# Attention with 120- and 96-row key tiles, and products over all 128 partitions, ahead of two MoE layers

## Chip, core and metric

One NeuronCore of a Trainium2 chip runs the whole kernel in one launch. The metric is the device time of the launch in microseconds; the times below are the median of three runs and their spread. The engines are named as in the profile: PE is TensorE (matmuls), PEld its weight loads, DVE VectorE, ACT ScalarE, POOL GpSimd, SP SyncE, which issues most DMAs.

## What is computed

The input has 4 batches x 8 heads x 576 tokens x 64 dimensions of q, k and v, and one score `s` per head and token. Only the first third of the reference matters here, the attention:

```python
scores = scale * np.matmul(q, k.transpose(0, 1, 3, 2))
cum = np.cumsum(np.maximum(s, 0.0), axis=-1)
bias = -(cum[:, :, :, None] - cum[:, :, None, :])
scores = np.where(causal, -1000000000.0, scores + np.minimum(bias, 0.0))
scores = scores - np.max(scores, axis=-1, keepdims=True)
attn = np.exp(scores)
attn = attn / (np.sum(attn, axis=-1, keepdims=True) + 1e-09)
return np.matmul(attn, v)
```

Its output goes through an FFN (512 to 2048 to 512), and that through eight experts with a routing of 288 tokens each. Both come after attention and are not touched.

## The kernel before

**Heads and pairs.** `Attention.run` (L383) goes over 33 steps `n`, one per head and one more; two heads are a pair `p`. Step `n` computes the scores and row maxima of head `n`, the values of head `n-1`, and then the exponentials of head `n`. Odd steps are odd heads. The order of the work on every engine is written out by hand: each engine runs its instructions in the order of the code, waiting where an operand is not there yet.

**Operands.** Products are exact to more than one fp32r pass: q is split into a high and a low part, X = (high, low), Z holds the high part and rows for the bias and the maxima, Y and W hold the same of k. `prep_hi` (L191) brings a pair's q or k, both heads side by side, from rows to columns with five transposes on TensorE into the PSUM tile `pt`: one of 64 rows (keys 512 to 575), four of 128 (keys `4a + r` of partition `a`). ScalarE copies the high parts out (L219, L221, L207), VectorE makes the low ones (L230, L233, `prep_lo`). For k a DMA on the GpSimd queue copies the high part to the other half of Y (L211). k of the next pair is prepared in even steps after the fourth score tile, q at the end of even steps.

**Scores and maxima.** `rows_max` (L236) computes six score tiles of up to 448 columns: a product over 128 rows (L249) and one over 96 (L250) each. VectorE takes row maxima (L252, L256) into `m`, one column per tile of queries; the first tile has 64 queries, so rows 64 to 127 of its column keep the zeros of the set-up. `nm` is made of them in two steps (L258, L259). `rows_put` (L262, "the put") turns the maxima into rows with five products against the identity (L271), one per tile of queries, the first over 64 rows, and ScalarE copies them into Z (L272). The PSUM tiles of scores, exponentials and put share four buffers in turn (tag `s`).

**Exponentials and values.** `exps` (L275) recomputes the scores by key tiles, with masks as products (`mu`), and ScalarE writes exp of them to E (L305). `values` (L313) multiplies E with V and a block of ones, key tile by key tile, in fp32, which gives two products per call (L333). The last key tile has 64 keys; its rows of E and V are cut to 64. The order in a step is: score tiles 1 to 4, then (odd steps) the first two value blocks, score tiles 5 and 6, more values, the put, the values of key tiles 3 and 4, then the exponentials.

**Loads.** `load` (L166) fetches q, k and v of four heads at a time on the SP queue, some 5 heads ahead, spread over steps: for q and k four DMAs of 512 rows (128 partitions x 4 rows) and one of 64 rows of all four heads.

**Beside it.** The FFN's weights come as 64-bit numbers. `Ffn.side` (L526) converts one block per step: two steps on DVE (L494, L495), one on ACT (L498), two on DVE (L500, L502), one on ACT (L504), a multiply on POOL (L505), a DMA to DRAM (L523). These stand in the same queues as attention's work.

**Set-up.** `setup` (L58) fills constants, among them the ones in V on GpSimd (L119), ahead of GpSimd's first copy into Z (L149).

Of the kernel before, what the change touches and what calls it, by code (L numbers as in the profile page):

```python
# [33 lines left out]
class Attention:  # L34
# [23 lines left out]
    def setup(self, identf):  # L58
        nc, c = self.nc, self.c
        S = self.S  # L60
        self.identf = identf
        st = self.w.tile([32, S], F32, name="s_in", tag="El")
        nc.scalar.dma_start(st, self.s.rearrange("b h s -> (b h) s"))
        self.load_first(0)
        zero = c.tile([128, 128], F32, name="zero")
        one = c.tile([128, 1], F32, name="one")
        nc.vector.memset(zero, 0.0)
        nc.vector.memset(one, 1.0)
        self.identb = c.tile([128, 128], BF16, name="identb")
        nc.vector.tensor_copy(self.identb, identf)  # L70

        self.ml = c.tile([128, 576], BF16, name="ml")
        self.mu = c.tile([128, 128], BF16, name="mu")
        nc.gpsimd.memset(self.ml[:, :448], 0.0)
        nc.gpsimd.affine_select(self.ml[:, 448:], zero, pattern=[[-1, 128]], compare_op=OP.is_ge, fill=-1e30,
                                base=0, channel_multiplier=1)
        nc.gpsimd.affine_select(self.mu, zero, pattern=[[1, 128]], compare_op=OP.is_ge, fill=-1e30,
                                base=0, channel_multiplier=-1)
        self.stacks, self.vbuf, self.mcol = [], [], []
        for i in range(2):  # L80
            X = c.tile([128, 2, S], F32R, name=f"X{i}")
            Y = c.tile([128, 2, 640], F32R, name=f"Y{i}")
            Z = c.tile([128, 2, S], F32R, name=f"Z{i}")
            W = c.tile([128, 2, 640], F32R, name=f"W{i}")
            V = c.tile([128, 5, 2, 3, 64], F32, name=f"V{i}")
            m = c.tile([128, 6], F32, name=f"m{i}")
            self.stacks.append((X, Y, Z, W))
            self.vbuf.append(V)
            self.mcol.append(m)
            nc.vector.memset(m, 0.0)  # L90

        zb, ob = zero[:, 0:1], one
        dve = lambda o, x: nc.vector.tensor_copy(o, x)
        gps = lambda o, x: nc.gpsimd.memset(f(o), 0.0 if x is zb else 1.0)

        def fill(o, x, cp):
            if cp is not gps:
                r = o.shape
                x = x[o.start_partition():o.start_partition() + r[0]]
                x = (x[:, :, None] if len(r) == 3 else x).to_broadcast(list(r))  # L100
            cp(o, x)

        act = lambda o, x: nc.scalar.activation(o, x, AF.Copy)

        def fill_w(i):
            X, Y, Z, W = self.stacks[i]
            for o, x, cp in ((W[64:128], zb, act), (W[96:98, :, :S], ob, act), (Y[:, :, S:], zb, dve),
                             (W[0:64, :, S:], zb, dve)):
                fill(o, x, cp)

        def fill_z(i, cp):
            Z = self.stacks[i][2]
            for o, x in ((Z[64:128], zb), (Z[64:66], ob)):
                fill(o, x, cp)

        fill_w(0)
        fill_z(0, gps)
        for V in self.vbuf:
            nc.gpsimd.memset(V[:, :, :, 1], 1.0)  # L119
        self.prep_hi(0, 1)  # L120
        self.prep_hi(0, 0)
        cum = self.w.tile([32, S], F32, name="cum", tag="El")
        nc.vector.tensor_scalar(st, st, 0.0, None, op0=OP.max)
        nc.vector.tensor_tensor_scan(cum, st, st, 0.0, op0=OP.add, op1=OP.bypass)
        ck = self.w.tile([32, 2, S], F32R, name="ck", tag="Eh")
        nc.vector.tensor_copy(ck[:, 0], cum)
        nc.vector.tensor_tensor(ck[:, 1], cum, f(ck)[:, 0], op=OP.subtract)
        X, Y, Z, W = self.stacks[0]
        for h in range(2):
            nc.sync.dma_start(f(W)[64:66, h, :S], f(ck)[h:h + 1])  # L130
        self.ckd = self.dr.tile([32, 2, S], F32, name="ckd")
        nc.sync.dma_start(self.ckd, f(ck))
        self.load_first(1)
        self.first_pair(0)
        fill_z(1, gps)
        fill_w(1)
        self.identr = c.tile([128, 128], F32R, name="identr")
        nc.vector.tensor_copy(self.identr, identf)
        for j in range(10, 15):
            self.load(0, j)  # L140

        self.rd = self.dr.tile([self.B * self.H, S], F32, name="rd")
# [11 lines left out]
    def load_first(self, p):  # L154

        for name in "kq":
            if p == 0:
                t = self.ld.tile([128, 5, 4, 64], F32, name="n" + name)
                self.nat[name, 0] = t[:, :, 0:2]
                self.nat[name, 1] = t[:, :, 2:4]  # L160
            t, s = self.nat[name, p], getattr(self, "qs" if name == "q" else name)[0, 2 * p:2 * p + 2]
            for h in range(2):
                self.nc.sync.dma_start(t[:, 0:4, h], s[h, 0:512].rearrange("(p r) d -> p r d", r=4))
            self.nc.sync.dma_start(t[:64, 4], s[:, 512:576].rearrange("h p d -> p h d"))

    def load(self, g, j):  # L166

        nc = self.nc
        if 2 * g >= self.NP:
            return  # L170
        name, r = "kqv"[j // 5], j % 5
        b, h0 = divmod(4 * g, self.H)
        s = getattr(self, "qs" if name == "q" else name)[b, h0:h0 + 4]
        if name == "v":
            rows = s[:, r * 128:min(r * 128 + 128, self.S)]
            t = self.vbuf[g % 2][:rows.shape[1], r]
            for i in range(2):
                nc.sync.dma_start(t[:, i, 0::2], rows[2 * i:2 * i + 2].rearrange("h p d -> p h d"))
            return
        if r == 0:  # L180
            t = self.ld.tile([128, 5, 4, 64], F32, name="n" + name)
            self.nat[name, 2 * g] = t[:, :, 0:2]
            self.nat[name, 2 * g + 1] = t[:, :, 2:4]
            self.nt = t
        t = self.nt
        if r == 4:
            nc.sync.dma_start(t[:64, 4], s[:, 512:576].rearrange("h p d -> p h d"))
        else:
            nc.sync.dma_start(t[:, 0:4, r], s[r, 0:512].rearrange("(p r) d -> p r d", r=4))

    def prep_hi(self, p, which):  # L191

        nc, S = self.nc, self.S
        x = self.nat["qk"[which], p]
        pt = self.pt[which] = self.ps.tile([128, 1024], F32, name="pt", tag="t" if p or which else "o")
        nc.tensor.transpose(pt[:, 512:576], x[:64, 4].rearrange("p h d -> p (h d)"),
                            self.identf[:64, :64])
        for r in range(4):
            nc.tensor.transpose(pt[:, 0:512].rearrange("p (a r) -> p r a", r=4)[:, r, :],  # L199
                                x[:, r].rearrange("p h d -> p (h d)"), self.identf)  # L200
        if p == 0:
            return
        X, Y, Z, W = self.stacks[p % 2]
        self.copy_hi(p, which, (0, 1))
        if which == 0:
            for h in range(2):
                nc.scalar.activation(Z[0:64, h], self.pt[0][64 * h:64 * h + 64, :S], AF.Copy,  # L207
                                     scale=1.0 / math.sqrt(self.D))
        else:
            nc.gpsimd.dma_start(f(W)[64:66, :, :S], self.ckd[2 * p:2 * p + 2].rearrange("h r s -> r h s"))  # L210
            nc.gpsimd.dma_start(f(Y)[64:128, :, :S], f(Y)[0:64, :, :S])  # L211

    def copy_hi(self, p, which, heads):
        nc, S = self.nc, self.S
        X, Y, Z, W = self.stacks[p % 2]
        for h in heads:
            src = self.pt[which][64 * h:64 * h + 64, :S]
            if which == 0:
                nc.scalar.activation(X[0:64, h], src, AF.Copy, scale=1.0 / math.sqrt(self.D))  # L219
            else:  # L220
# [2 lines left out]
    def prep_lo(self, p, which, heads=(0, 1)):  # L223
# [1 line left out]
        nc, S = self.nc, self.S  # L225
        X, Y, Z, W = self.stacks[p % 2]
        for h in heads:
            src = self.pt[which][64 * h:64 * h + 64, :S]
            if which == 0:
                nc.vector.scalar_tensor_tensor(X[64:128, h], src, 1.0 / math.sqrt(self.D), f(X)[0:64, h],  # L230
                                               op0=OP.mult, op1=OP.subtract)
# [30 lines left out]
    def rows_put(self, n, nm):  # L262
# [3 lines left out]
        for q0, tiles in ((0, self.QT[:4]), (448, self.QT[4:])):  # L266
            t = self.ps.tile([128, 512], F32, name="pr", tag="s", bufs=4)
            for a, b in tiles:
                i = self.QT.index((a, b))
                m = b - a  # L270
                nc.tensor.matmul(t[:2, a - q0:b - q0], nm[:m, i, :], self.identr[:m, :m], start=True, stop=True)  # L271
            nc.scalar.activation(Z[96:98, n % 2, q0:b], t[:2, :b - q0], AF.Copy)  # L272


# [38 lines left out]
    def values(self, n, mid=None):  # L313
# [6 lines left out]
        for (g0, g1), order in zip(((0, 256), (256, 576)), self.VALUES):  # L320
# [3 lines left out]
            for i, w in enumerate(order):  # L324
                if w == "|":
                    if mid:
# [3 lines left out]
                a, b = self.KT[kb]  # L330
                c0 = max(a, g0)
                e0 = self.ECOL[kb] + c0 - a
                nc.tensor.matmul(t[:, 256 + c0:256 + g1], V[:b - a, kb, 64 * h:64 * h + 128],  # L333
                                 E[:b - a, e0:e0 + g1 - c0], start=i == 0, stop=i == len(order) - 1)
        self.evac = lambda: self.out(n, t)
        if n < 2 * self.NP - 1:
            self.evac()
# [1315 lines left out]
```

## Time and profile before

| | |
|---|---|
| median of 3 runs | 1049.25 us (1046.25 to 1054.68) |
| the profiled execution | 1042.44 us |
| its span, first to last instruction | 1040.7 us |
| mean granted clock of TensorE | 0.98 of full speed |
| TensorE busy (matmuls) | 968.7 us, 93% |
| VectorE busy | 790.0 us, 76% |
| ScalarE, GpSimd busy | 489.3 us (47%), 455.1 us (44%) |

All durations come from the one profiled execution. "Busy" is the time in which an engine has an instruction under way; matmuls overlap each other, and their ends are modelled, so the distance from start to start says more than a duration. A weight load can run while the matmul ahead of it streams. A row of the time order has the start, the duration, the engine, the line, output and inputs, and in brackets the idle time ahead and what ended it; x2 is two instructions that follow each other. Attention is the first 289 us of the span.

### The profile page before, as it was taken

The page shows a single profiled execution, that of the slowest core. Times are in us where ns is not written, and L with a number is a line of the kernel's source. Part 1 is how long each engine was busy: PE and PEld are TensorE (multiplying, and loading weights), DVE is VectorE, ACT ScalarE, POOL GpSimd, SP SyncE. Part 2 cuts the span into 40 slices and gives each one's busy share as a digit, 9 for nine tenths or more (in the row PEclk, how much of TensorE's full clock was granted, in tenths as well). Part 3 has the DMA queues.
Part 4 walks back from the last instruction along what each step waited for, and adds up shares of the span by engine and source line. Part 5 has one row for each costly group of instructions (what it writes and reads, how often), then busy time and mean ns, then how long its engine had stood idle before and what let it go on. Part 6 is the DMA issues. An engine that isn't in the chain of part 4 may idle for free.

```text
span 1040.7 us, 18588 instructions
## 1 busy us (share of the span) xinstructions
PE 968.7 (93%) x6479; PEld 856.2 (82%) x6479; DVE 790.0 (76%) x2029; ACT 489.3 (47%) x961; POOL 455.1 (44%) x471
## 2 busy tenths in 40 slices
PE   6899999999989999999899899999899979989996
PEld 5777777777768899888798798889788878879996
DVE  6688888988857667999999999885576687766510
ACT  5677777777745532322322322430245435536531
POOL 3245454445423233424424333330668868973211
PEclk9999999999999999999899899999899989999999
DMA  5767777878566040020020110101645455557400
GB/s 129 166 163 200 184 205 188 218 189 214 165 212 232 2 172 1 1 91 1 6 87 1 53 39 0 62 1 42 198 136 164 132 169 166 167 147 236 127 24 24
DMA packets 123067, 122.66 MB, mean 118 GB/s; under 512 B 73922, under 2 KB 90562, under 8 KB 122844
## 3 DMA queue, kind: packets, MB, share of 16 engines
q1 hardware_dynamic: 104604, 89.79, 30.8%
q0 software_dynamic: 17312, 30.55, 10.1%
q10 hardware_dynamic: 1056, 1.12, 0.4%
q8 instruction: 51, 0.84, 0.3%
q14 instruction: 44, 0.36, 0.1%
HBM read 89.36 MB, written 27.50 MB: 112 GB/s over the span
## 4 chain that ended last, share of the span: by engine, by line
PE 66%; DVE 22%; issue 5%; DMA 3%; ACT 2%; POOL 2%; SPq 0%; another core or an unknown queue 0%; POOLq 0%; DVEq 0%; ACTq 0%
PE ph L619 11%; PE py L1486 8%; PE ph L1434 8%; DVE junk L677 7%; PE po L333 6%; PE pst L301 6%; PE px L656 4%; PE px L658 4%; PE px L657 4%; PE ps L249 2%; DVE cmp L1212 2%; PE ps L250 2%; PE rp L1121 2%; PE pt L199 2%; DVE nm L259 2%
## 5 line engine op out<-in xcount | busy, mean ns | idle before, releaser
L641 POOL TENSOR_TENSOR gl<-u,gh 128x384 fp32r<-128x384 f32 x80 | 98.4, 1230 | 237.1 <-ACT gh L640 152.6
L1212 POOL TENSOR_TENSOR wl<-raw,wh 128x512 fp32r<-128x512 f32 x98 | 129.4, 1346 | 59.6 <-DMA raw<-in_moe_w_dram 33.8
L628 ACT ACTIVATE u<-u,half 128x384 f32<-128x384 f32 x96 | 59.2, 617 | 183.4 <-DVE u L627 180.9
L619 PE MATMUL ph<-xh,ih 128*128 128x384 f32 x384 | 132.2, 344 | 7.4 <-ACT xh L605 4.2
L619 PE MATMUL ph<-xl,ih 128*128 128x384 f32 x384 | 132.4, 345 | 4.1 <-DVE xl L606 4.1
L619 PE MATMUL ph<-xh,il 128*128 128x384 f32 x384 | 132.3, 345 | 3.0 <-DVE il L591 2.9
L677 DVE SCALAR_TENSOR_TENSOR junk<-wt,gb 128x512 f32<-128x512 f32 x128 | 116.7, 947 | 0.0
L333 PE MATMUL po<-E,V 128*128 128x320 f32 (+4 forms) x448 | 112.6, 379 | 0.4 <-ACT E L305 0.4
L677 DVE SCALAR_TENSOR_TENSOR junk<-x,gb 128x512 f32<-128x512 f32 x120 | 103.0, 888 | 4.5 <-ACT x L665 4.5
L656 PE MATMUL px<-oh,gh 128*128 128x512 f32 x240 | 96.0, 400 | 1.7 <-ACT x L665 1.7
L658 PE MATMUL px<-oh,gl 128*128 128x512 f32 x240 | 96.6, 402 | 0.7 <-POOL gl L641 0.7
L657 PE MATMUL px<-ol,gh 128*128 128x512 f32 x240 | 95.4, 398 | 0.0
L333 PEld LDWEIGHTS po<-E,V 128*128 128x128 f32 (+1 forms) x448 | 74.9, 191 | 20.1 <-issue 7.4
L619 PEld LDWEIGHTS ph<-xh,ih 128*128 128x128 f32 x384 | 73.5, 192 | 13.8 <-ACT xh L605 5.9
L1486 PE MATMUL py<-hh,wh 128*128 128x288 f32 x256 | 81.1, 317 | 0.0
L619 PEld LDWEIGHTS ph<-xl,ih 128*128 128x128 f32 x384 | 73.7, 192 | 8.7 <-DVE xl L606 5.2
L1212 ACT ACTIVATE wh<-raw 128x512 fp32r<-128x512 f32 x128 | 76.0, 623 | 9.2 <-DMA raw<-in_moe_w_dram 8.3
L1434 PE MATMUL ph<-xh,wh 128*128 128x288 f32 x256 | 79.1, 309 | 0.2 <-ACT xh L1212 0.2
L1434 PE MATMUL ph<-xl,wh 128*128 128x288 f32 x256 | 78.5, 307 | 0.5 <-DVE xl L1212 0.4
L1434 PE MATMUL ph<-xh,wl 128*128 128x288 f32 x256 | 78.1, 305 | 0.0
L619 PEld LDWEIGHTS ph<-xh,il 128*128 128x128 f32 x384 | 73.6, 192 | 4.8 <-DVE il L591 4.8
L1486 PE MATMUL py<-hl,wh 128*128 128x288 f32 x256 | 77.3, 302 | 0.0
(228 smaller groups left out, 2513.3 us busy)
## 6 DMA issues: line engine op xcount, KB each, us to landing
raw<-in_moe_w_dram SPq DMA_DIRECT2D x128, 256.0 KB
r<-in_moe_w_in_dram SPq DMA_DIRECT2D x16, 512.0 KB
r<-in_moe_w_out_dram SPq DMA_DIRECT2D x16, 512.0 KB
xg<-xd SPq DMA_DIRECT2D x6, 768.0 KB
x2d<-x SPq DMA_DIRECT2D x36, 128.0 KB
Y<-Y POOLq DMA_DIRECT2D x15, 288.0 KB
nk<-in_k_dram SPq DMA_DIRECT2D x32, 128.0 KB
nq<-in_q_dram SPq DMA_DIRECT2D x32, 128.0 KB
```

What stands on the lines that cost most here:

```text
L301: nc.tensor.matmul(pst[u][:, cols], l, r, start=first, stop=last, skip_group_check=u == "c" or u == "b")
L333: nc.tensor.matmul(t[:, 256 + c0:256 + g1], V[:b - a, kb, 64 * h:64 * h + 128], E[:b - a, e0:e0 + g1 - c0], start=i == 0, stop=i == len(or ...
L619: nc.tensor.matmul(p[:, :G], a[:, s], b, start=n == 0, stop=n == 11)
L628: nc.scalar.activation(u, u, AF.Square, bias=self.half, scale=0.5)
L641: (nc.vector if keep and i == self.NF - 1 else nc.gpsimd).tensor_tensor(gl, u, f(gh), op=OP.subtract)
L656: nc.tensor.matmul(px[t][:, cols], gh[:, s], oh[:, cols], start=i == 0, stop=False)
L657: nc.tensor.matmul(px[t][:, cols], gh[:, s], ol[:, cols], start=False, stop=False)
L658: nc.tensor.matmul(px[t][:, cols], gl[:, s], oh[:, cols], start=False, stop=last)
L677: self.nc.vector.scalar_tensor_tensor(junk, x(), 1.0, self.gb[:, e], op0=OP.mult, op1=OP.mult, accum_out=out[:, e:e + 1])
L1212: return fn(*a, **kw)
L1434: self.nc.tensor.matmul(p[:, :self.C], a[:, cols], b, start=c == 0 and i == 0, stop=c == 3 and i == 2)
L1486: nc.tensor.matmul(p[:, :C], a[:, o:o + 128], b[:, fb], start=fb == 0 and i == 0, stop=fb == 7 and i == 2)
```

## The change

Queries and keys are cut so that no tile has 64 rows. q and k arrive as 480 rows on 120 partitions (4 each) and 96 rows on 96 partitions, and the transposes are four of 120 rows and one of 96; the columns of `pt` begin at 32 instead of 0, so that the last 96 lie behind column 512. The values' last key tile keeps its 64 keys but contracts over all 128 partitions: V's rows 64 to 127 of that tile are set to zero once, and E's rows there were computed before too, as exponentials of masked scores. The put contracts over 128 partitions for the first tile of queries too, whose padding rows are zeros. The remaining calls and their order stay.

```diff
@@ setup
         for V in self.vbuf:
             nc.gpsimd.memset(V[:, :, :, 1], 1.0)
+
+            nc.gpsimd.memset(V[64:, 4], 0.0)
@@ load_first
-                self.nc.sync.dma_start(t[:, 0:4, h], s[h, 0:512].rearrange("(p r) d -> p r d", r=4))
-            self.nc.sync.dma_start(t[:64, 4], s[:, 512:576].rearrange("h p d -> p h d"))
+                self.nc.sync.dma_start(t[:120, 0:4, h], s[h, 0:480].rearrange("(p r) d -> p r d", r=4))
+            self.nc.sync.dma_start(t[:96, 4], s[:, 480:576].rearrange("h p d -> p h d"))
@@ load
-            nc.sync.dma_start(t[:64, 4], s[:, 512:576].rearrange("h p d -> p h d"))
+            nc.sync.dma_start(t[:96, 4], s[:, 480:576].rearrange("h p d -> p h d"))
         else:
-            nc.sync.dma_start(t[:, 0:4, r], s[r, 0:512].rearrange("(p r) d -> p r d", r=4))
+            nc.sync.dma_start(t[:120, 0:4, r], s[r, 0:480].rearrange("(p r) d -> p r d", r=4))
@@ prep_hi
-        nc.tensor.transpose(pt[:, 512:576], x[:64, 4].rearrange("p h d -> p (h d)"),
-                            self.identf[:64, :64])
+
+        nc.tensor.transpose(pt[:, 512:608], x[:96, 4].rearrange("p h d -> p (h d)"), self.identf[:96, :96])
         for r in range(4):
-            nc.tensor.transpose(pt[:, 0:512].rearrange("p (a r) -> p r a", r=4)[:, r, :],
-                                x[:, r].rearrange("p h d -> p (h d)"), self.identf)
+            nc.tensor.transpose(pt[:, 32:512].rearrange("p (a r) -> p r a", r=4)[:, r, :],
+                                x[:120, r].rearrange("p h d -> p (h d)"), self.identf[:120, :120])
...
-                nc.scalar.activation(Z[0:64, h], self.pt[0][64 * h:64 * h + 64, :S], AF.Copy,
+                nc.scalar.activation(Z[0:64, h], self.pt[0][64 * h:64 * h + 64, 32:32 + S], AF.Copy,
@@ copy_hi, prep_lo
-            src = self.pt[which][64 * h:64 * h + 64, :S]
+            src = self.pt[which][64 * h:64 * h + 64, 32:32 + S]
@@ rows_put
-                nc.tensor.matmul(t[:2, a - q0:b - q0], nm[:m, i, :], self.identr[:m, :m], start=True, stop=True)
+                nc.tensor.matmul(t[:2, a - q0:b - q0], nm[:, i, :], self.identr[:, :m], start=True, stop=True)
@@ values
-                nc.tensor.matmul(t[:, 256 + c0:256 + g1], V[:b - a, kb, 64 * h:64 * h + 128],
-                                 E[:b - a, e0:e0 + g1 - c0], start=i == 0, stop=i == len(order) - 1)
+                nc.tensor.matmul(t[:, 256 + c0:256 + g1], V[:, kb, 64 * h:64 * h + 128],
+                                 E[:, e0:e0 + g1 - c0], start=i == 0, stop=i == len(order) - 1)
```

## Rows read from the trace of the kernel before

**Rows 1.** The page, part 4: the chain that ended last, by engine.

```profile
PE 66%; DVE 22%; issue 5%; DMA 3%; ACT 2%; POOL 2%; SPq 0%; another core or an unknown queue 0%; POOLq 0%; DVEq 0%; ACTq 0%
```

**Rows 2.** Stretches: us, busy PE, PEld, DVE, ACT, POOL, clock, DMA share, GB/s.

```profile
197.99:214.85 16.86, 16.14 (x107) 12.93 (x107) 14.56 (x42) 12.80 (x25) 8.07 (x11) 1.00 0.82 204
206.59:213.43 6.84, 6.84 (x47) 5.81 (x46) 4.96 (x19) 6.64 (x14) 1.32 (x3) 1.00 0.80 211
```

**Rows 3.** Chain of waits, 0 to 300: first and last of thirteen odd puts.

```profile
63.07 0.52 PE pr L271 x5
...
265.42 0.52 PE pr L271 x5
```

**Rows 4.** Waits between them: us in total, times, longest.

```profile
PE pr L271 <- DVE nm L259: 8.5, 12, 0.7
...
PEld po L333 <- issue: 5.4, 24, 0.2
...
PEld pt L196 <- issue: 4.6, 24, 0.2
```

**Rows 5.** Time order, PE and PEld, step 22: values' last key tile.

```profile
206.66 0.33 PE L333 MATMUL po<-E,V 128*128 128x192 f32 x1
...
206.92 0.29 PEld L333 LDWEIGHTS po<-E,V 64*128 64x128 f32 x2 [0.23 <-issue]
...
207.28 0.19 PEld L301 LDWEIGHTS pst<-X,Y 128*128 128x128 f32 x1
```

**Rows 6.** Time order, PE and PEld, step 22: transposes of q.

```profile
209.15 0.30 PE L301 MATMUL pst<-Z,W 128*128 128x320 f32 x1
...
209.38 0.14 PEld L196 LDWEIGHTS pt<-identf,nq 64*128 64x128 f32 x1 [0.19 <-issue]
...
209.87 0.14 PEld L199 LDWEIGHTS pt<-identf,nq 128*128 128x128 f32 x1
209.97 0.19 PEld L249 LDWEIGHTS ps<-Y,X 128*128 128x128 f32 x1
```

**Rows 7.** Time order, PE and PEld: the puts of steps 22 and 23.

```profile
205.73 0.43 PE L333 MATMUL po<-E,V 128*128 128x320 f32 x1
206.09 0.08 PEld L271 LDWEIGHTS pr<-identr,nm 64*2 64x2 f32 x1 [0.44 <-issue]
...
213.43 0.70 PE L333 MATMUL po<-E,V 128*128 128x320 f32 x2
214.85 0.19 PE L271 MATMUL pr<-identr,nm 64*2 64x64 f32 x1 [0.72 <-DVE nm L259]
215.15 0.19 PEld L333 LDWEIGHTS po<-E,V 128*128 128x128 f32 x1
```

**Rows 8.** Time order, DVE and POOL: `nm` in steps 3, 22 and 23.

```profile
45.70 0.17 DVE L259 TENSOR_TENSOR nm<-m,nm 128x5 fp32r<-128x5 f32 x1
45.71 1.30 POOL L505 TENSOR_TENSOR co<-cm,ce 128x512 f32<-128x512 f32 x1 [4.72 <-issue]
...
205.19 0.17 DVE L259 TENSOR_TENSOR nm<-m,nm 128x5 fp32r<-128x5 f32 x1
...
213.51 1.26 POOL L505 TENSOR_TENSOR co<-cm,ce 128x512 f32<-128x512 f32 x1 [3.92 <-ACT cm L504]
213.56 1.24 DVE L259 TENSOR_TENSOR nm<-m,nm 128x5 fp32r<-128x5 f32 x1
```

**Rows 9.** Weight loads by shape, 200 to 210: count, busy us, mean ns, idle before.

```profile
L250 PEld LDWEIGHTS ps<-W,Z 96*128 96x128 f32 x5 | 0.9, 190 | 0.0
```

**Rows 10.** Time order, DVE and PE, step 22: second and sixth score tile.

```profile
203.28 0.14 DVE L252 DVE_READ_ACCUMULATOR2_ANT m<- 128x1 f32 x1
...
203.56 0.20 PE L249 MATMUL ps<-Y,X 128*64 128x64 f32 x1
```

**Rows 11.** Time order, POOL: set-up's memsets of V and the next copy.

```profile
5.11 1.21 POOL L119 MEMSET V<- 128x640 f32 x2
9.14 0.66 POOL L149 TENSOR_SCALAR Z<-X 64x576 fp32r<-64x576 f32 x1 [2.82 <-ACT X L219]
```

## What I expect, and why

> **What bounds the kernel now.** I read the page first. The chain that ended last is 66% TensorE and 22% VectorE, so a shorter TensorE stream moves the end wherever TensorE ends last [rows 1]. The change touches only attention, so I went to the table of stretches there. In one pair of heads (197.99 to 214.85 us) TensorE is busy 16.14 of 16.86 us at the full granted clock, VectorE 14.56, ScalarE 12.80, and the DMA engines 0.82 of the time [rows 2]. The chain of waits shows how regular this is: the product that turns the maxima around (L271, "the put") of every odd head stands in it every 16.86 us, (265.42 - 63.07) / 12 [rows 3]. Between these marks the chain is TensorE, except at the odd put, where VectorE takes over: twelve times TensorE waits 0.7 us for the maxima `nm` [rows 4].
>
> The list of waits also holds what the change is about. The weight loads of L333 and L196 stand still 24 times each for about 0.2 us with "issue" as releaser: nothing that the profile shows ended that wait [rows 4]. In time order these are the loads of 64 rows. A load of 128 rows starts while the matmul ahead is streaming; one of 64 rows starts only when the matmul ahead has drained, and the next one of 128 rows again waits for it [rows 5, 6]. Loads of 96 rows (L250) show no idle time, 0.0 over five [rows 9]. So 96 and 120 rows should behave as 128.
>
> **The change part by part.** First what goes, per occurrence.
>
> Values, last key tile (2 products, each head): the last 192-column product starts at 206.66 and the load after the two 64-row products at 207.28, 0.62 later [rows 5]. Without draining, 192 columns stream in 0.16: a 320-column one takes 0.27, since two of them span 0.70 and one alone 0.43 [rows 7], and 0.27 x 192 / 320 = 0.16. The two small products then go at the pace of their weight loads, 0.11 each (209.87 to 209.97 and its like) [rows 6]; the second load is also the start of the next one, so 0.16 + 0.11 = 0.27. Saved 0.34.
>
> Transposes (5 products, twice per pair): from the last score product at 209.15 to the load behind the transposes at 209.97 it is 0.82 now. After: one 320-column product in a single pass, 320 / 2.4 GHz = 0.13, at this clock [rows 2] and with the start of the next some 0.14, and four load times of 0.11: 0.58. 96 and 120 moving columns stay under a load time, so they add nothing. Saved 0.24. If loads of 120 rows were to drain as those of 64 do, nothing here would be saved; the 96-row rows speak against it.
>
> The put (first of 5 products, each head): in even heads it begins 0.36 after the 320-column product at 205.73, instead of 0.27: 0.09 saved. Leaving it, five loads take 0.30 (214.85 to 215.15); without the drain behind the first about 0.085 less, as the other loads follow at some 0.06 and a 64-column product is half as long [rows 7]. In odd heads only that 0.085 counts, since TensorE waits for `nm` at its start anyway.
>
> Per pair: 2 x 0.34 + 2 x 0.24 + 0.175 + 0.085 = 1.42 us.
>
> Then what this sets off. The odd head's second step of `nm` (L259) takes 1.24 us instead of 0.17 because GpSimd's multiply of a weight block (L505, 1.26) started 0.05 before it, and VectorE's instruction ended with it. In step 3 the same two started 45.70 and 45.71, VectorE first, and L259 took 0.17 [rows 8]. L505 waits for ScalarE [rows 8], which is busy 6.64 of the 6.84 us between the even put's copy and that moment [rows 2], so L505 keeps its distance from that put; L259 follows the scores, which come earlier by 0.34 + 0.24 = 0.58. So L259 ends before L505 begins, and the maxima are there before TensorE wants them. TensorE would then go on at 213.97 instead of 214.85 (the 320-column products that start at 213.43, two times 0.27) [rows 7]: 0.88 more per pair. Sum: 16.86 - 1.42 - 0.88 = 14.56.
>
> What is late next. (a) In even heads VectorE starts on the scores when its queue of weight conversions lets it, not when they come. The sixth score tile takes the buffer that VectorE released at 203.42, 0.14 before its product at 203.56 [rows 10]; TensorE gains 0.085 + 0.34 + 0.24 = 0.66 up to there; VectorE gains 0.2, because it ends `nm` about 0.24 before the odd put then, 0.05 now. Some 0.35 (0.66 - 0.2 - 0.14, rounded up for the semaphore) comes back as a wait. (b) In odd heads the scores reach buffers that ScalarE's exponentials free: about 0.1. (c) The DMA engines: 0.82 x 16.86 = 13.8 us of work per pair [rows 2] would be 0.92 of 15.0. The lower end is 0, since 13.8 still fits (below it is excluded: no transfer goes away); the upper end is 0.9, where late loads of the weight blocks that VectorE converts eat the whole 0.88. I take 0.4, because the loads come in bursts and 0.92 leaves little time to catch up. `nm` of the even head has slack: it ends at 205.36 [rows 8] against 206.09, and about 0.75 of gain before that put uses it up, which (a) covers. So a pair takes 14.56 + 0.35 + 0.1 + 0.4 = 15.4, 1.45 less; twelve pairs give 17.4.
>
> Ends: heads 2 to 4 wait for nothing and save 0.34 + 0.24 + 0.175 each, 2.3; the head before 63.07 about 1.5 (0.34 + 0.24 + 0.085 + 0.88); after 265.42 two puts and three heads of values, 1.8. Together 5.6; all in all 23 us.
>
> Added work. Two memsets of 64 x 384 on GpSimd in the set-up: between 0 and the 0.6 of the 128 x 640 ones each (I take 0.35). They lie in the 2.82 us that GpSimd waits behind those for ScalarE [rows 11]; without that cover 0.7 us would fall on the first pair. DMAs keep their number and bytes; four of each five carry 480 rows over 120 partitions, the fifth 96 rows instead of 64. A third more in the fifth and 6% less in the four: between -0.1 and +0.1 us per load; I take 0. Where these are split over fewer engines, see the third rival. No wait is added, and the FFN begins with loads issued behind attention, so its start moves along.
>
> The profiled execution took 1042.44 us (span 1040.7), 6.8 below the median of the runs shown. It would come to 1019.5; the prediction is made for the median: 1049.25 - 23 = 1026.
>
> **The rivals.**
> 1. The 0.88 stays: another wait takes the place of the one removed (L259 still under L505, or the weight conversions on VectorE waiting for their DMA). For: VectorE has 14.56 of busy time per pair, and 13.5 when 1.07 of L259 goes, so it follows TensorE closely [rows 2]. Against: step 3 [rows 8]. Then even put to odd put goes from 8.76 to 8.67 only, odd put to even put from 8.10 to 7.35 (0.085, 0.34, 0.24, 0.09): 16.0 per pair, 12 x 0.84 + 4.7 = 15 saved: 1034.
> 2. No new wait at all: 14.56 per pair, 12 x 2.3 + 5.6 = 33 saved: 1016.
> 3. Slower: the 480-row loads run on few DMA engines. Place: SP's loads of q and k. Eight of 128 KB in two pairs are 1.05 MB; an engine moves 204 / 0.82 / 16 = 15.5 GB/s when busy [rows 2], so they take 4.2 us of each engine, and on five engines 13.5. These then have 27.6 + 9.3 = 36.9 us of work in two pairs that take 33.7, 3.2 more; six times that is 19: 1068. It decides from some seven engines down; at eight, 31.8 per two pairs would still be a gain (about 1032). For: 120 is not a multiple of 16. Against: nothing in the trace of before shows such a load. The Trainium skill (DMA: Bandwidth & Descriptors, Why a DMA increments its semaphore by 16 and not by 1) says that a DMA takes the largest number of engines up to 16 that divides its slowest dimension: 15 for 120, 16 for 96. By that, each engine gets 32 rows as now, and this rival falls; no run here shows it yet.
> 4. Nothing: the 0.2 us belongs to these instructions and not to their 64 rows, and a padded product costs what the short one did; 1049. For: "issue" names no cause [rows 4]. Against: three lines with different operands show it, and the load after them too [rows 5 to 7]. The Trainium skill (TensorE: Matmul & The Clock Gate, What overlaps and what doesn't) says that a weight load overlaps a running matmul only where its row group differs. By that, padding would gain nothing or lose, 1049 or later. The trace differs: loads of 128 rows overlap matmuls of 128 rows (the load of 209.97 begins 0.04 before the one of 209.87 ends, and both while transposes stream [rows 6]).
>
> **How the numbers follow.** Forecast 0.56, rival 1 0.18, rival 2 0.10, rival 3 0.05 (and 0.03 for its mild form near no gain), rival 4 0.08. A measurement of this kernel tells about 1% from no change, 10.5 us. Faster by more: forecast, rivals 1 and 2, 0.84. Within: rival 4 and the mild 0.03, 0.11. Slower: 0.05. The range goes from rival 2 less 2 us to rival 1 plus 6, since the runs shown differ by 8 us: 1014 to 1040. It leaves out rivals 3 and 4, 0.16, and little beside.
>
> **What would show it.** Right: no 64-row form in L333, L271 and L196; no "issue" idle of their loads; 0.27 instead of 0.62 behind the 192-column product; odd puts every 15.4 us; L259 0.17 in odd heads; new waits of L249 for L252. Wrong: L259 at 1.2 again with odd puts every 16.0 (rival 1); idle VectorE ahead of L494 or TensorE ahead of L196 that a DMA ended (rival 3, or (c) too small); idle loads at 96 or 120 rows (rival 4).

## The result: no gain, 0.6% slower

The changed kernel takes 1056.49 us (median of 20 runs, 1048.18 to 1062.71) against 1050.41 us of the kernel before in as many runs (1041.03 to 1054.93): a ratio of 1.0057, interval 1.0035 to 1.0079. The forecast was 1026 with a range of 1014 to 1040, so the time lies outside. The profiled execution took 1055.52 us with a span of 1053.8, 13 us more than that of before, with 10.0 of them there at the last put of attention (291.14 below, 281.17 before). The 13 are more than the 6 between the medians, as the profiled execution of before is 8 us below its median. The new lines stand two or three further down: L271 is L273 now, L333 is L335, L259 is L261, L249 is L251; the transposes are L199 (96 rows) and L201 (120 rows), the loads of 480 rows L191 and of 96 rows L189.

First the page, part 4 of the kernel after, the chain that ended last by engine; DMA was 3% in [rows 1].

```profile
PE 52%; DVE 23%; DMA 12%; issue 6%; ACT 3%; SPq 2%; POOL 2%; POOLq 0%; DVEq 0%; ACTq 0%
```

Then the chain of waits of the kernel after from 0 to 300 us (start, length, what): odd puts, and between them the pieces of over 10 us on a DMA.

```profile
46.92 0.27 PE pr L273 x5
...
76.34 0.27 PE pr L273 x5
...
96.22 12.53 DMA nq<-in_q_dram
...
118.63 13.86 DMA r<-in_moe_w_in_dram
...
135.99 13.00 DMA r<-in_moe_w_in_dram
...
167.70 12.99 DMA nq<-in_q_dram
...
190.56 14.01 DMA r<-in_moe_w_in_dram
...
208.34 12.86 DMA r<-in_moe_w_in_dram
...
240.33 13.85 DMA nq<-in_q_dram
...
276.20 0.27 PE pr L273 x5
...
291.14 0.27 PE pr L273 x5
```

There are two halves. Up to 84 us the kernel does what was forecast, and more: an odd put takes 0.27 instead of 0.52 [rows 3], and from 46.92 two pairs take 29.42 us, 14.7 each instead of 16.86. Behind 84 us the chain runs seven times through a transfer of 12.5 to 14 us: three times the last load of a head's q (`nq`), four times a block `r` of the FFN's weights, which VectorE converts during attention. The list of waits of the kernel after (85 to 250 us: us in total, times, longest) says who stands still for them. In the kernel before no wait of this stretch was ended by a DMA; those of TensorE on which the forecast rests are in [rows 4].

```profile
DVE ce L496 <- DMA r<-in_moe_w_in_dram: 12.7, 7, 3.1
...
PE pt L199 <- DMA nq<-in_q_dram: 5.9, 2, 3.1
...
DVE ce L496 <- DMA r<-in_moe_w_out_dram: 4.5, 1, 4.5
```

One would look for DMA engines that have no room left. The table of stretches (us, busy PE, PEld, DVE, ACT, POOL, clock, DMA share, GB/s) says the contrary. Here is 88 to 250 us of the kernel before:

```profile
88.00:250.00 162.00, 154.89 (x1018) 124.01 (x1018) 139.41 (x391) 123.32 (x242) 76.29 (x104) 1.00 0.79 197
```

and the same of the kernel after, with four single microseconds of it:

```profile
88.00:250.00 162.00, 144.81 (x945) 122.38 (x943) 121.69 (x367) 114.57 (x222) 71.37 (x99) 0.94 0.73 187
...
97.00:98.00 1.00, 0.00 (x0) 0.00 (x0) 0.97 (x3) 0.88 (x2) 0.17 (x1) 1.00 0.89 282
...
100.00:101.00 1.00, 1.00 (x3) 0.66 (x3) 0.93 (x7) 0.00 (x0) 0.97 (x2) 0.50 1.14 271
...
104.00:105.00 1.00, 1.00 (x12) 0.92 (x12) 0.39 (x2) 0.95 (x4) 0.00 (x0) 1.00 0.11 39
...
107.00:108.00 1.00, 0.00 (x0) 0.00 (x0) 0.00 (x0) 0.27 (x1) 0.00 (x0) 1.00 0.68 215
```

The mean DMA share fell, 0.79 to 0.73, while the kernel waits for DMAs. The row of 104 us is the clue: the share is 0.11, which is 1.8 engines of 16, and the load of q for which TensorE waits until 108.75 is under way. Two engines are working, and fourteen have nothing to do. In the trace's packet records this microsecond holds eight packets of 4608 bytes and eight of 256: two rows of `R` against one row of q, in turn. The issues stand on the timeline of POOL (first view) and of SP (second; start, length, engine, line) in the kernel after.

```profile
94.20 0.83 POOL L377 DMA_DIRECT2D R<-rd  x1 [0.43 <-issue]
```

```profile
96.22 0.75 SPq L189 DMA_DIRECT2D nq<-in_q_dram  x1
```

L377 copies the two heads' 1/sums to 128 partitions: `to_broadcast([2, 64, S])`, 288 KB whose slowest dimension is the two heads. Its sixteen completions: fourteen by 100.3, the last two at 105.7 and 105.9. The q load, issued 2.02 us behind it: fourteen by 101.8, the last two only at 107.06 and 108.75. The kernel before had the same copy, and there also two completions were late (issued 200.75, last one 212.3). But its q loads went ahead of it, here on the timeline of the kernel before:

```profile
200.16 0.63 SPq L187 DMA_DIRECT2D nq<-in_q_dram  x1
200.75 0.84 POOL L375 DMA_DIRECT2D R<-rd  x1
```

That load landed at 206.37 and was wanted at 209.39.

The Trainium skill (DMA: Bandwidth & Descriptors, Why a DMA increments its semaphore by 16 and not by 1) says that a DMA uses the largest number of engines up to 16 that divides the slowest dimension of both its sides, and that one issued by GpSimd takes consecutive engines in turn. By that, `R` has two engines and a load of 120 partitions has 15. The trace agrees with both: two late completions for `R`; and a load of 480 rows (issued at 95.31) has 15 completions where the others have 16.

### The profile page after: what moved, and what is told of

Read it like the earlier page. It is cut to its first block, busy times and chain, and to the rows that moved or that the text cites. A ratio compares the mean times of both kernels' runs of the same rounds, so it can differ in the third digit from the quotient of the medians.

```text
span 1053.8 us, 18590 instructions
## 1 busy us (share of the span) xinstructions
PE 964.9 (92%) x6479; PEld 864.6 (82%) x6479; DVE 778.9 (74%) x2029; ACT 490.1 (47%) x961; POOL 456.4 (43%) x473
## 4 chain that ended last, share of the span: by engine, by line
PE 52%; DVE 23%; DMA 12%; issue 6%; ACT 3%; SPq 2%; POOL 2%; POOLq 0%; DVEq 0%; ACTq 0%
DVE junk L679 9%; PE ph L1436 8%; PE py L1488 8%; PE ph L621 8%; PE po L335 5%; DMA r<-in_moe_w_in_dram 5%; DMA nq<-in_q_dram 4%; PE px L658 4%; PE px L660 3%; PE px L659 3%; PE pst L303 3%; DVE cmp L1214 2%; PE ps L251 2%; PE rp L1123 2%; DVE u L641 2%
## 5 line engine op out<-in xcount | busy, mean ns | idle before, releaser
L335 PE MATMUL po<-E,V 128*128 128x320 f32 (+4 forms) x448 | 115.2, 396 | 0.4 <-ACT E L307 0.4
L335 PEld LDWEIGHTS po<-E,V 128*128 128x128 f32 x448 | 81.8, 206 | 15.1 <-issue 2.9
L251 PE MATMUL ps<-Y,X 128*128 128x320 f32 (+2 forms) x192 | 65.5, 353 | 14.8 <-DVE m L258 7.8
L507 POOL TENSOR_TENSOR co<-cm,ce 128x512 f32<-128x512 f32 x32 | 41.6, 1299 | 85.8 <-ACT cm L506 81.0
```

The costliest lines, as they stand in the source:

```text
L251: nc.tensor.matmul(t[:m, :w], X[:, h, a:b], Y[:, h, c0:c1], start=True, stop=False)
L335: nc.tensor.matmul(t[:, 256 + c0:256 + g1], V[:, kb, 64 * h:64 * h + 128], E[:, e0:e0 + g1 - c0], start=i == 0, stop=i == len(order) - 1)
```

## The experiments

**Theory A:** `R` on two engines is the bound as soon as pairs take 15 us. **Theory B:** it is the new geometry of the loads of q and k (120 partitions, 15 engines, longer issues). The first four runs ask which of them it is.

**Only the products** (e1): loads and transposes as before, values and put over 128 rows, the padding of V with them.

```diff
-nm[:m, i, :], self.identr[:m, :m]
+nm[:, i, :], self.identr[:, :m]
-V[:b - a, kb, ...], E[:b - a, ...]
+V[:, kb, ...], E[:, ...]
+nc.gpsimd.memset(V[64:, 4], 0.0)
```

> The loads and transposes of before, with the values' last key tile and the put over 128 rows. Theory A (the DMAs were bound to two engines: the copy of the reciprocal sums R to all partitions goes over two DMA engines, and once the pairs come closer together the loads of q and of the weight blocks fall behind it on these two): the pairs shrink by 0.94 plus the freed 0.88, and waits for DMAs of q or r appear as after the change, 1045 to 1058. Theory B (the new shape of the loads is slow: 480 rows on 120 partitions, issued in 0.87 us instead of 0.62, and 96 packets per head instead of 64 in the tail): no DMA waits, pairs of 15 to 15.5, 1028 to 1035.

Measured: 1049.4 us, ratio 1.0016 (0.9975 to 1.0058). The chain of waits of this run, 85 to 250 us:

```profile
94.60 13.95 DMA nq<-in_q_dram
...
136.28 12.60 DMA r<-in_moe_w_in_dram
...
165.37 10.80 DMA nq<-in_q_dram
...
203.84 13.12 DMA r<-in_moe_w_in_dram
```

The loads of before, with their 128 partitions, are waited for in the same way. So the new geometry isn't needed for these waits, and the products alone gain nothing either.

**Only loads and transposes** (e2): the kernel after with the two products of before.

```diff
-nm[:, i, :], self.identr[:, :m]
+nm[:m, i, :], self.identr[:m, :m]
-V[:, kb, ...], E[:, ...]
+V[:b - a, kb, ...], E[:b - a, ...]
```

> The loads and transposes of after, with the values and the put of before. Theory A: the transposes give 0.48 per pair and L259 is freed from L505 too, so the pairs come nearly as close and the same waits appear, 1048 to 1058. Theory B: the slow loads remain and the gain of the products is gone, 1055 to 1065.

Measured: 1059.07 us, ratio 1.0093 (1.0059 to 1.0127). Here the chain of waits (85 to 250 us) has q alone:

```profile
96.10 14.98 DMA nq<-in_q_dram
...
170.64 13.71 DMA nq<-in_q_dram
...
242.15 15.48 DMA nq<-in_q_dram
```

Before these its odd puts stood 15.5 us apart (45.91, 61.40, 76.92), so this half shortens the pair too, and that is enough to bring the waits about. The time itself lies 1 us above the range of theory A and inside that of theory B, so this run does not tell the two apart.

**Loads of 512 rows on 128 partitions** (e3): all of the change, but the four tiles of q and k are loaded over all partitions, and the transposes read 120 of them.

```diff
-t[:120, 0:4, r], s[r, 0:480].rearrange("(p r) d -> p r d", r=4)
+t[:, 0:4, r], s[r, 0:512].rearrange("(p r) d -> p r d", r=4)
```

> As after, but the four big loads bring 512 rows on 128 partitions again (the transposes read 120 of them) and the fifth stays at 96 rows. Theory A: as after, 1052 to 1060, with q landing 10 us and more behind its issue. Theory B: issue time back to 0.62 us, most waits for DMAs gone, 1028 to 1040.

Measured: 1052.53 us, ratio 1.0033 (0.9994 to 1.0071), which its interval does not tell from the change itself. The waits for `r` and q remain (11.0 us in seven and 9.7 us in three, 40 to 290 us). What the geometry does cost stands in the rows of tile `nk` (duration in ns, min/median/max): the issue on SP of the kernel after,

```profile
L191 SPq DMA_DIRECT2D nk<-in_k_dram x28: 849/885/6726, 19.9 to 224.4; - x28
```

and with 512 rows:

```profile
L191 SPq DMA_DIRECT2D nk<-in_k_dram x28: 562/628/6327, 18.9 to 220.9; - x28
```

The medians differ by 0.26 us per load in SP's queue: a real cost, and a small one. The longest of each row, over 6 us in both, is another matter, and comes back in e4.

**`R` in two DMAs of 64 partitions** (e4): all of the change, and

```diff
-self.q.dma_start(R, self.rd[n:n + 2, None, :].to_broadcast([2, 64, S]))
+for h in range(2):
+    self.q.dma_start(R[64 * h:64 * h + 64], self.rd[n + h:n + h + 1, :].to_broadcast([64, S]))
```

> As after, but R is copied with two DMAs of 64 partitions each, one per head, instead of one whose outermost dimension is 2. Theory A: the two slow DMA engines are gone, q and r land together on all engines, pairs of 14.8 to 15.4 throughout, 1020 to 1032. Theory B: R has nothing to do with it, 1052 to 1060.

Measured: 1021.53 us, ratio 0.9734 (0.9659 to 0.9809). The table of stretches, 88 to 250 us:

```profile
88.00:250.00 162.00, 161.20 (x1146) 140.08 (x1146) 146.12 (x448) 136.91 (x268) 89.32 (x129) 1.00 0.89 223
```

TensorE is busy 161.20 of 162 us, the clock is full, and the DMA share is 0.89: higher than in the two kernels above, with nothing on the path waiting for it. The copies issued at 108.27 and 108.78 have their sixteen completions within 0.5 and 0.7 us. The chain of waits has no DMA between 32 and 262 us, and its odd puts stand 14.95 apart:

```profile
120.65 0.27 PE pr L273 x5
...
135.60 0.27 PE pr L273 x5
...
255.19 0.27 PE pr L273 x5
```

Something else goes with the two-engine copy: the stand-still of SP's queue. Here the issues of q's loads on SP (tile `nq`, same columns as for `nk`), first in the kernel before, then in the kernel after, then in e4:

```profile
L189 SPq DMA_DIRECT2D nq<-in_q_dram x28: 540/706/7867, 23.8 to 232.9; - x28
```

```profile
L191 SPq DMA_DIRECT2D nq<-in_q_dram x28: 849/866/7987, 24.7 to 239.4; - x28
```

```profile
L191 SPq DMA_DIRECT2D nq<-in_q_dram x28: 849/866/1259, 24.8 to 205.6; - x28
```

An issue takes up to 8 us where `R` is one DMA, and 1.3 us at most in e4. So the load of q that goes out at 96.22 in the kernel after goes out at 86.91 in e4, ahead of the copy of `R` and not behind it. The queue stood still in the kernel before too. What such an issue waits for, the profile does not say.

The next four ask whether the split helps by itself, and whether the geometry matters once `R` is out of the way.

**The kernel before with `R` split** (e5), by the diff of e4.

> Before, with R copied by two DMAs of 64 partitions. Theory A: before did not wait for the two engines, so the pairs stay at 16.9 and L259 at 1.24 us: 1044 to 1052. Rival (R's copy held up before too): 1035 or less.

Measured: 1047.92 us, ratio 0.9973 (0.9938 to 1.0009). At 16.86 us per pair `R` held up nothing on the path; what it costs appears in the time only when pairs come closer. SP's queue did gain: its longest issue of a load of q is 1.9 us here and 7.9 in the kernel before.

**512 rows and `R` split** (e6: e3 and e4 together).

> After with 512-row loads on 128 partitions and the split R. Theory A with the load's issue as a separate small cost (64 DMAs, 0.25 us more each in SP's queue, about 1.1 us of it on the start): 1017 to 1022, 1 to 3 us faster than the split R alone. If the shape of the loads matters as much as without the split: 1012 to 1016.

Measured: 1020.69 us, ratio 0.972 (0.9694 to 0.9746), as e4. Theory B has nothing left that these runs can measure.

**Only the products, `R` split** (e7: e1 and e4 together).

> Before's loads and transposes, values and put over 128 rows, split R. Theory A: a pair loses 0.94 and the 0.88 of the odd put, less some 0.4 of waits for buffers, so 15.4 per pair and 12 x 1.45 + 4 = 21 less: 1025 to 1031.

Measured: 1022.17 us, ratio 0.9749 (0.9717 to 0.978), better than expected. The pair, by the odd puts in its chain of waits, is longer than in e4, 15.27 instead of 14.95:

```profile
122.84 0.27 PE pr L272 x5
...
138.11 0.27 PE pr L272 x5
```

So the transposes give 0.32 per pair, some 4 us in all (12 x 0.32); against the loads' longer issues and their later first q these can't be told apart in the time.

**`R` in two DMAs by columns** (e8): again two DMAs, but each of both heads, so that the slowest dimension stays 2.

```diff
+for c in (slice(0, S // 2), slice(S // 2, S)):
+    self.q.dma_start(R[:, c], self.rd[n:n + 2, None, c].to_broadcast([2, 64, S // 2]))
```

> As after, but R is copied with two DMAs of half the columns each, whose outermost dimension is still 2. Theory A (what counts is that a copy with outermost 2 runs on two engines): if both halves fall on the same two engines, 1052 to 1060; if on two pairs of engines, half the backlog on twice the engines, 1030 to 1050. Rival (two DMAs instead of one are what helped): 1018 to 1026, as with the split by heads.

Measured: 1024.34 us, ratio 0.9775 (0.9753 to 0.9798). By its time this speaks for the rival "two DMAs are better than one": theory A had expected 1030 at the least. In the completions (copies issued at 94.12 and 94.96) two of the first and four of the second are late, by 2.6 to 4.0 us only. That could be theory A with the halves on different pairs of engines and half the bytes on each (four late ones are the two of the first copy and two more), or the number of DMAs. VectorE still waits for `r` here, 4.2 us in five times from 85 to 250 us, where the kernel after has 12.7 in seven and e4 none. The last two runs separate these.

**A further copy on two engines** (e9) and **the same bytes over all engines** (e10). Both are e4 with one more copy of the same rows into a tile that nobody reads, which is work added:

```diff
+R2 = self.nw.tile([128, S], F32, name="R2", bufs=1)
+self.q.dma_start(R2, self.rd[n:n + 2, None, :].to_broadcast([2, 64, S]))      # e9
+for h in range(2):                                                            # e10
+    self.q.dma_start(R2[64 * h:64 * h + 64], self.rd[n + h:n + h + 1, :].to_broadcast([64, S]))
```

> The kernel with R copied in two DMAs of 64 partitions (1021.5 us) and, behind them, one more copy of the same rows into a tile that nobody reads, made as R was: one DMA whose slowest dimension is the two heads. Theory A (a copy of this shape loads two engines only, and what falls behind them on these, the loads of q and of the weight blocks, sets the pair): the waits for q and r come back although R itself is early: 1040 to 1062 us, TensorE idle ahead of the transposes of q or VectorE ahead of the conversions for over 10 us in sum. Rival (R came late because it was one DMA, and two are better whatever engines they use): R is two DMAs still, and the third is read by nobody: 1020 to 1030, no such waits.

> The same additional bytes as in the run beside it, but as two DMAs of 64 partitions, as R itself is copied there. Theory A: about 295 KB more over 16 engines is 1.2 us more of each engine's time per pair (at 15.5 GB/s of an engine), which the pair of 15 us mostly takes: 1021 to 1032 us, waits for q or r of under 5 us in sum. Rival (the DMA engines have no room left for any more bytes in a pair of 15 us): the waits come back here too, 1035 to 1060, as in the run beside it.

Measured: e9 1072.28 us, ratio 1.0201 (1.0126 to 1.0276), above the range that theory A gave; e10 1024.44 us, ratio 0.9765 (0.9707 to 0.9822), inside it. The stretch of 88 to 250 us in e9,

```profile
88.00:250.00 162.00, 135.04 (x883) 115.99 (x882) 116.03 (x346) 108.36 (x211) 73.80 (x106) 0.93 0.79 190
```

its waits there,

```profile
DVE ce L499 <- DMA r<-in_moe_w_in_dram: 16.0, 5, 4.3
...
POOL R L378 <- DMA rd<-r: 13.2, 5, 3.4
...
PE ps L251 <- DMA Y<-Y: 9.0, 4, 3.6
...
PE pt L199 <- DMA nq<-in_q_dram: 5.4, 1, 5.4
```

and the stretch in e10:

```profile
88.00:250.00 162.00, 160.17 (x1134) 138.51 (x1132) 147.93 (x440) 135.80 (x268) 100.33 (x152) 1.00 0.99 240
```

The copy in one DMA costs 48 us more than the same bytes in two, and nobody reads it. Its harm is to others: q, `r`, the copied high parts of k (`Y`) and the rows of 1/sums are what TensorE, VectorE and GpSimd wait for. In e10 no wait from 85 to 250 us is ended by a load of q or `r`. The DMAs are more in e10 and the share is 0.99, and TensorE is still busy 160 of 162 us. So a copy on two engines is shown to be the cause, as theory A has it, and the count of DMAs is not. The 48 us contain both its ways of harm, the late packets on two engines and SP's queue (an issue of a load of q takes up to 8.7 us in e9, 2.0 in e10); no run separates them, though e8 is fast with issues of up to 5.9.

## Why the prediction was wrong, step by step

- **Values, transposes, put: right.** The 64-row forms are gone, loads of 96 and 120 rows show no idle time (e4), and pairs take 14.7 us in the kernel after as long as no DMA is late; so rival 4 is out. The transposes are worth 0.32 per pair by e7 against e4, where 0.48 stood.
- **The 0.88 of L259: right.** At the put TensorE waited for `nm` 7.1 us in ten times before (85 to 250 us), and not once in the kernel after or in e4. All 32 of them are short now, here of the kernel after (ns, min/median/max), where [rows 8] has 1.24 us:

```profile
L261 DVE TENSOR_TENSOR nm<-m,nm x32: 166/166/168, 15.4 to 290.3; 128x5 fp32r<-128x5 f32 x32
```

- **New waits: (a) there and smaller, (b) not seen.** 14.56 + 0.35 + 0.1 was forecast ahead of the DMA term; e4 shows 14.95, so 0.39 over 14.56 for all that is late, and for what the transposes fell short of. The 64-column loads of L251 wait 0.12 each for L254 (0.5 us over four, 120 to 150 us in e4), where 0.35 stood. No wait of L251 for ScalarE's exponentials stands in e4's list of 85 to 250 us.
- **(c), the DMA engines: the step that failed.** It took the mean share of 16 engines, 0.82 of 16.86 us, as work that fits into 15 us, and gave 0.4 for bursts, 0.9 at most. What it measured: from the odd put at 61.62 to that of 276.20 twelve pairs take 214.58 us, 17.9 each, where e4 shows 14.95: 3 us per pair. A mean over engines doesn't see a transfer that lies on two of them. `R` is 64 packets of 4608 bytes: 32 on each of two engines at about 0.19 us (packet records of the kernel after), 6 us even if nothing else is there, and longer with q's packets in between; spread over 16 it is four each, 0.8 us. And the 0.92 that the step feared does no harm: e4 runs at 0.89 and e10 at 0.99.
- **What it looked past.** For L375 no DMA was asked on how many engines it runs; the question was asked of the new loads alone (rival 3). There the answer was right: 120 partitions did not become the bound (e3, e6). The mechanism of rival 3, few engines, was at work in a DMA that the change doesn't touch. The sign that the prediction named, VectorE or TensorE idle until a DMA, is what came.
- **480-row loads at 0: too low.** Each issue takes 0.26 us more on SP, and the first transposes of q start at 8.18 instead of 6.95 us. In the time it is below what e3 and e6 can tell.
- **Slips without weight.** 0.62 - 0.27 is 0.35 and not 0.34; the 1.8 after 265.42 comes to 1.4 from its own items (2 x 0.175 + 3 x 0.34); 96 rows in the fifth load are half more than 64, not a third. Together they are below 1 us.
- **Sum.** With `R` spread, the change gives 1048.4 - 1021.5 = 27 us (against the kernel before as measured beside e4) where 23 were forecast. By the last put the profiled executions are 26.0 apart (281.17 to 255.19), at the end 18.1 (spans 1040.7 and 1022.6): that of before is one of its shortest, that of e4 the longest of four.

Why the waits cost more than the gain, so that the kernel became slower and not just stayed equal, was not taken apart by a run. The trace of the kernel after shows where the time lies: of the twelve pairs, three take 23.8, 24.6 and 25.5 us from odd put to odd put, the other nine 14.6 to 18.2. In these three q's last load was issued 1.7 to 2.8 us behind a copy of `R` (at 96.22, 167.70 and 240.33), and TensorE waited 2.8 to 4.2 us for it. Where it was issued ahead (133.25 and 204.70), TensorE did not wait for it. In e1 and e2 too, each q load on the chain from 85 us on was issued behind a copy; in e3 two of three. In the kernel before it always went ahead. No run moved the order alone. Another contribution is the clock: when TensorE has waited (nothing at 97 us), it is granted 0.50, the 1.2 GHz level, at 100 us, and the mean clock over 88 to 250 us is 0.94 instead of 1.00.

The version to keep is the change with `R` copied in two DMAs of 64 partitions: 1021.5 us, 2.7% below the kernel before and some 3% below the kernel after. With loads of 512 rows (e6) it is the same within the intervals.

## What to carry to other kernels

Where a step shortens the period of a loop, ask of each DMA in that loop, also of those that the change leaves alone, over how many engines it is spread: the broadcast whose slowest dimension is 2 sat on two engines here, and what was queued behind it there came late. The mean DMA share could not tell; look at completions that come in two groups, at stretches of 1 us in which the share drops to one or two sixteenths, at issues that take microseconds, and at waits that end with small loads issued long before. The repair may cost one line: cut such a copy into DMAs that each have a large slowest dimension (64 here).

## What the runs showed of the hardware

- A copy on two engines isn't free for the others. In the packet records each `R` of the kernel after comes with 448 packets of 8 bytes beside its 64 of 4608, 32 for each of the fourteen other engines if they share evenly; split in two (e4) these are gone. By themselves they are not the cause: e8 brings 448 small ones per copy too (of 16 bytes), at 1024.3 us. On the page's part 3 the queue of GpSimd's DMAs shrinks with that, here the kernel after and then e4:

```profile
q0 software_dynamic: 17312, 30.55, 9.8%
```

```profile
q0 software_dynamic: 11264, 30.51, 9.9%
```

That is 6048 packets less for 14 copies, 432 each: 448 less the 16 completions of the additional DMA.

- The DMA share can be above 1 in a microsecond (1.14 at 100 us) and 0.99 over 162 us with TensorE busy for 160.17 of them (e10). So it can't be read as how full the engines are: it adds up the time that packets took.
- A load of 480 rows over 120 partitions takes 0.26 us longer to issue on SP than one of 512 rows over 128 (medians of 885 and 628 ns).
- Issues on SP stood still for up to 6 to 9 us in every run with a two-engine copy (5.9 in e8, which is fast even so), and the longest of q's loads took 0.9 to 2.0 us in the five runs without one (e4 to e7, e10).
